# Accumulator copies on VectorE, attention's copies at a higher priority, and two of six weight tiles rounded beside the attention

## The chip, the cores and the metric

The kernel runs on one NeuronCore of a Trainium2 chip: TensorE (PE) multiplies, VectorE (DVE), ScalarE (ACT) and GpSimd (POOL) do the elementwise work, SyncE (SP) issues the DMAs. The metric is the device time of one execution, in microseconds (us); smaller is better.

## The reference, cut to what matters

Windowed attention with a linear position bias on 4 batches of 8 heads, 576 positions, head dimension 64, and then two gated feed-forward layers on the 2304 tokens, all in fp32:

```python
scores = scale * np.matmul(q, k.transpose(0, 1, 3, 2))
scores = np.where(mask, scores + bias[None], -1e9)      # mask: 0 <= q - k < 128
attn = softmax(scores)
x = np.matmul(attn, v)                                  # laid out as [2304, 512]
x = (sigmoid(x @ w_gate) * (x @ w_val)) @ w_out         # 512 -> 1536 -> 512
y = (((x @ w1) * (x @ w2)) @ w3) @ w_out2               # 512 -> 1024 -> 1024 -> 512
```

## The kernel before, in words

**Precision.** A product of two fp32 matrices is made of three matmuls on pairs of a high and a low part (`PASSES`), each part in the type that TensorE takes at full rate. So every operand is split: a copy that rounds makes the high part (`act_copy`, on ACT), a subtraction the low part (`dve_lo` on DVE, `pool_lo` on POOL). The weights come from memory as 64-bit words, 512 KB for a tile of 128x512; `rounded` (L110) turns such a tile into fp32 with one instruction on ACT (L116) and six on DVE (L117 to L122). `convert_next` (L125) takes the next tile of a queue: it rounds it if need be and then either splits it into the weight buffer `wsl` (one ACT copy, one POOL subtraction) or, for an "ahead" tile, writes the fp32 values to a DRAM scratch `early32` (L132), from where a later fetch reads 256 KB of plain fp32. Each call fetches the tile after the next. Buffers of the raw words (`raw`), of the result (`ca`) and of the scale (`cs`) are two each. Conversions run at a priority 300 instructions later than their place in the program (`LATER`).

**Order.** Tokens are in five blocks of 2, 4, 4, 4 and 4 tiles of 128. The attention takes 20 steps (block times pair of heads). Step n issues `stage_p(n-2)` (transposes `pt`, copied to `cp` on ACT at L487, then two selects on POOL), `stage_pv(n-3)` (product `pv`, split into `xt` by ACT and DVE at L514 and L515) and `stage_s(n)` (scores `s`; L450, L453, L459 on DVE, eight exponentials L466 on ACT, L474 on POOL). PE's order in the attention is written out by hand. The other engines' orders come from a planner that takes the ready instruction of the best priority by its own clock; on the chip every engine then works through its queue in that order, so an instruction that waits holds up all behind it. `tc.high_priority(offset=SOONER)` puts an instruction 150 places ahead.

**Fillers.** Between the steps PE gets pieces of the first feed-forward layer for the first group of two hidden tiles: `gv` (the gate and value products, L244; sigmoid on ACT L259, the product of both on DVE L266, its split on ACT and POOL) and `down1` (L283), whose four PSUM tiles `dn` per block go to the accumulator `acc`: the first group copies (L291, on ACT), later groups add on DVE (L293). `FILL` and `READY` say how much and which block at which step. `CONVERT` (L527) says how many tiles `convert_next` takes at a step: twelve in all, six for the first group (hidden tiles 0 and 1) and the six "ahead" tiles of the second group (hidden tiles 2 and 3 of `w_gate`, `w_val`, `w_out`, L192).

**After the attention.** The rest of the fillers runs while the second group's six tiles are fetched and split (L599 to L605); its weight buffers lie where the attention's were. From then on each group is a round of some 74 us over the five blocks, in which DVE, ACT and POOL convert the next group's six tiles and five ahead tiles (`w_out2`, `w3` and others) beside it.

Of the kernel before, what the change touches and what calls it, by code (L numbers as in the profile page):

```python
# [32 lines left out]
SOONER = 150  # L33
# [13 lines left out]
def attn_moe_kernel(  # L47
# [14 lines left out]
    nc = tc.nc  # L62
# [6 lines left out]
    def act_copy(dst, src):  # L69
        nc.scalar.activation(dst, src, AF.Copy)  # L70

    def dve_lo(dst, src, hi):
        nc.vector.tensor_tensor(dst, src, hi.bitcast(F32), ALU.subtract)  # L73
# [13 lines left out]
    def cols(blk):  # L87
        return TILES[blk] * P

    def x_tile(name, blk):  # L90
        return xpool.tile([P, 2, NK, cols(blk)], F32R, name=f"{name}{blk}", tag=f"xb{blk}")

    def acc_tile(blk, shape, name):
        return accpools[blk > 1].tile(shape, F32, tag=f"acc{blk}", name=f"{name}_{blk}")
# [53 lines left out]
    groups = [tuple(range(i, i + GF)) for i in range(0, NF + NM, GF)]  # L148
# [40 lines left out]
    early = [it for it in fold_src if it[0][0] == "o2" or it[0][1] in W3_AHEAD]  # L189
    early += [((i, c), (w1, w2)[c][i - NF]) for c in range(2) for i in groups[NF // GF]]  # L190
    late_n = len(early)
    early += [((i, c), (w_gate, w_val, w_out)[c][i]) for c in range(3) for i in groups[1]]  # L192
    early32 = dpool.tile([P * len(early), DM], F32, name="early32")
    ahead = {key: early32[i * P : (i + 1) * P, :] for i, (key, _) in enumerate(early)}
    ahead_items = [(("ahead", *key), src, None) for key, src in early]
# [33 lines left out]
    def mm_tile(shape, name):  # L229
        mmturn[0] += 1  # L230
        return mmpools[mmturn[0] % len(mmpools)].tile(shape, F32, tag="mm", name=name)
# [40 lines left out]
    def down1(grp, blk, ts):  # L272
        first, last = grp[0] == 0, grp[-1] == NF - 1
        if first:
            acc[blk] = acc_tile(blk, [P, NK, cols(blk)], "acc1")
        if last:
            x2.append(x_tile("x2_", blk))
        for m in range(NK):
            ps = mm_tile([P, TB], f"dn{grp[0]}_{blk}_{m}")[:, 0 : cols(blk)]
            n = 0  # L280
            for i, t in zip(grp, ts):
                for wp, xp in PASSES:
                    nc.tensor.matmul(  # L283
                        ps, wsl[i][:, 2, wp, m * P : (m + 1) * P], t[:, xp],
                        start=n == 0, stop=n == 3 * len(grp) - 1,
                    )
                    n += 1
            a = acc[blk][:, m]
            with tc.high_priority(offset=SOONER):
                if first:  # L290
                    act_copy(a, ps)  # L291
                else:
                    nc.vector.tensor_tensor(a, a, ps, ALU.add)  # L293
            if last:
                act_copy(x2[blk][:, 0, m], a)
                dve_lo(x2[blk][:, 1, m], a, x2[blk][:, 0, m])
            yield 3 * len(grp) * (cols(blk) / 2.4 + 13.3)
# [36 lines left out]
    def attention(actx, conv):  # L334
# [60 lines left out]
        def where(n):  # L395

            blk, pair = divmod(n, NPAIR)
            return pair, blk, TILES[blk], STARTS[blk], min(blk, 1)
# [79 lines left out]
        def stage_p(n):  # L478
            pair, blk, nt, t0, back = where(n)
            s = st[n]  # L480
            for h in range(2):
                ps = gvpool.tile([P, 4, P], F32, tag="mm", name=f"pt{n}_{h}")
                for t in range(nt):
                    nc.tensor.transpose(ps[:, t], s["sm"][:, t // 2 * 2 + h, t % 2], ident)  # L484
                cp = ap2.tile([P, 4, 2, P], F32, tag="cp", name=f"cp{n}_{h}", bufs=4)
                own, prev = cp[:, 0:nt, 1], cp[:, 0:nt, 0]
                act_copy(own, ps[:, 0:nt])  # L487
                nc.gpsimd.affine_select(  # L488
                    out=prev, in_=own, compare_op=ALU.is_gt, fill=0.0, base=0,
                    pattern=[[0, nt], [-1, P]], channel_multiplier=1,  # L490
                )
                nc.gpsimd.affine_select(  # L492
                    out=own, in_=own, compare_op=ALU.is_ge, fill=0.0, base=0,
                    pattern=[[0, nt], [1, P]], channel_multiplier=-1,
                )
                s["cp", h] = cp.rearrange("p t c k -> p (t c k)")

        def stage_pv(n):
            pair, blk, nt, t0, back = where(n)
            s = st[n]  # L500
            ps = gvpool.tile([P, TB], F32, tag="mm", name=f"pv{n}")[:, 0 : nt * P]
            for j in range(-back, nt):
                a, b = max(j, 0) * P, min(j + 2, nt) * P
                m0 = 0 if j < 0 else (2 * j + 1) * P
                for h in range(2):
                    c = slice(h * D, (h + 1) * D)
                    nc.tensor.matmul(  # L507
                        ps[c, a:b], loads[n]["v"][:, j + 1, c], s["cp", h][:, m0 : m0 + b - a],
                        start=j == -back, stop=j == nt - 1, skip_group_check=True,
                    )  # L510
            if pair == 0:
                xt.append(x_tile("xt", blk))
            x = xt[blk]
            act_copy(x[:, 0, pair], ps)  # L514
            dve_lo(x[:, 1, pair], ps, x[:, 0, pair])  # L515

        def fill(budget):

            while fillers and budget > 0:
                cost = next(fillers[0], None)  # L520
                if cost is None:
                    fillers.pop(0)
                else:
                    budget -= cost


        CONVERT = {1: 1, 3: 1, 5: 1, 8: 1, 9: 1, 10: 1, 11: 1, 12: 1, 13: 2, 14: 2}  # L527

        READY = {
            5: (((0,), 0),), 10: (((0,), 1),), 12: (((1,), 0), ((1,), 1)), 14: (((0, 1), 2),), 18: (((0, 1), 3),),  # L530
# [2 lines left out]
            0: ((stage_s, 0),),  # L533
            1: ((stage_s, 1),),
            2: ((stage_s, 2), (stage_p, 0)),
            3: ((stage_s, 3), (stage_pv, 0), (stage_p, 1)),
            4: ((stage_s, 4), (stage_pv, 1), (stage_p, 2)),
            5: ((stage_p, 3), (stage_pv, 2), (stage_s, 5), (stage_pv, 3)),
            6: ((stage_p, 4), (stage_s, 6)),
        }  # L540
# [11 lines left out]
        with tc.manual_schedule(engines={mybir.EngineType.PE}):  # L552
            for n in range(NSTEP + 3):
# [20 lines left out]
                fill(FILL.get(n, FULL))  # L574
                for _ in range(CONVERT.get(n, 0)):
                    with tc.issue_after(st[n]["dve"].ins), tc.issue_after(st[n]["act"].ins):
# [3 lines left out]
    with ExitStack() as conv, ExitStack() as actx:  # L580
        attention(actx, conv)
# [110 lines left out]
```

## Time and profile before

| | us |
|---|---|
| median of three runs | 938.03 (937.9 to 939.07) |
| profiled execution | 936.87 |
| its span, first to last instruction | 935.2 |
| PE busy in the span | 897.4 (96%) |
| DVE, ACT, POOL busy | 565.1, 355.1, 311.6 |

The attention takes the first 197 us of the span. There PE has gaps; behind it PE is busy nearly without one. "Granted clock" is TensorE's clock as a share of 2.4 GHz. Matmuls overlap, so that the start of a row can lie a little before the end of the row above it. A bracket at the end of a timeline row gives the idle time of the engine just before it, and what ended it.

### The profile page before, as it was taken

To read this page: it belongs to the slowest core of one execution; us is meant where nothing else is said; L and a number is where in the kernel's file an instruction comes from. 1 tells how busy PE (TensorE), PEld (TensorE's weight loads), DVE (VectorE), ACT (ScalarE), POOL (GpSimd) and SP (SyncE) were. 2 spreads that over 40 slices of the span, in tenths; PEclk is the share of its full clock that TensorE was granted. 3 is DMA by queue.
4 is the path that set the end of the run, shared out by engine and by line. 5 is a ranking of instruction groups with operands and counts; after the bars stand their busy time and mean duration, and the time that the engine had idled before them with its cause. 6 is when DMAs were issued, how large, how long until landed. Compare 5 with 4: busy or idle time off the path is not lost.

```text
span 935.2 us, 12293 instructions
## 1 busy us (share of the span) xinstructions
PE 897.4 (96%) x4528; PEld 735.1 (79%) x4528; DVE 565.1 (60%) x945; ACT 355.1 (38%) x853; POOL 311.6 (33%) x408
## 2 busy tenths in 40 slices
PE   5889799899999999999999999999999999999998
PEld 2566677678878888888888888888888888888887
DVE  4867787417996996797783468833755524322223
ACT  5778777754322322322331334433322212211110
POOL 4877658452313312412421111104422412411111
PEclk9999899999999999999999999999999999999999
DMA  5544453014351251242130213234300300000113
GB/s 169 170 141 137 145 159 116 26 57 140 109 168 46 91 167 48 68 147 90 55 115 0 68 53 117 91 97 141 111 24 12 101 1 1 23 0 1 46 46 113
DMA packets 32604, 79.71 MB, mean 85 GB/s; under 512 B 3616, under 2 KB 5664, under 8 KB 32544
## 3 DMA queue, kind: packets, MB, share of 16 engines
q1 hardware_dynamic: 32544, 78.92, 26.2%
q8 instruction: 36, 0.59, 0.3%
q14 instruction: 24, 0.20, 0.1%
HBM read 65.27 MB, written 13.63 MB: 84 GB/s over the span
## 4 chain that ended last, share of the span: by engine, by line
PE 72%; DVE 8%; ACT 7%; POOL 6%; DMA 4%; issue 3%; SPq 0%; ACTq 0%; POOLq 0%; DVEq 0%
PE gv L244 43%; PE dn L283 11%; PE o L308 10%; PE w3o L210 4%; ACT sm L466 2%; POOL sm L474 2%; PE s L442 1%; PE pv L507 1%; POOL wsl L76 1%; PE pt L484 1%; POOL cp L488 1%; POOL cp L492 1%; ACT L466 1%; DVE sm L453 1%; DVE s L450 1%
## 5 line engine op out<-in xcount | busy, mean ns | idle before, releaser
L244 PE MATMUL gv<-xt,wsl 128*128 128x512 f32 (+1 forms) x1440 | 308.4, 372 | 7.8 <-ACT acc L70 4.0
L244 PEld LDWEIGHTS gv<-xt,wsl 128*128 128x128 f32 x1440 | 251.9, 190 | 58.2 <-ACT acc L70 4.5
L76 POOL TENSOR_TENSOR gt<-g,gt 128x512 fp32r<-128x512 f32 (+1 forms) x100 | 121.2, 1216 | 427.9 <-ACT gt L70 427.7
L244 PE MATMUL gv<-x,wsl 128*128 128x512 f32 (+1 forms) x960 | 200.2, 368 | 0.0
L244 PEld LDWEIGHTS gv<-x,wsl 128*128 128x128 f32 x960 | 167.6, 189 | 30.2
L266 DVE TENSOR_TENSOR g<-g,gv 128x512 f32<-128x512 f32 (+1 forms) x100 | 62.6, 630 | 168.4 <-PE gv L244 156.3
L283 PE MATMUL dn<-gt,wsl 128*128 128x512 f32 (+1 forms) x720 | 154.9, 369 | 2.4 <-ACT cp L70 1.2
L283 PEld LDWEIGHTS dn<-gt,wsl 128*128 128x128 f32 x720 | 125.7, 188 | 27.2 <-PE dn L283 1.8
L70 ACT ACTIVATE gt<-g 128x512 fp32r<-128x512 f32 (+1 forms) x100 | 58.4, 587 | 145.6 <-DVE g L266 145.6
L259 ACT ACTIVATE g<-gv 128x512 f32<-128x512 f32 (+1 forms) x100 | 54.8, 550 | 150.5 <-PE gv L244 146.4
L308 PE MATMUL o<-wsl,gt 128*128 128x512 f32 x432 | 101.1, 389 | 0.0
L308 PEld LDWEIGHTS o<-wsl,gt 128*128 128x128 f32 x432 | 80.9, 188 | 16.7
L293 DVE TENSOR_TENSOR acc<-acc,dn 128x512 f32<-128x512 f32 (+1 forms) x108 | 66.1, 622 | 20.7 <-PE dn L283 20.5
L474 POOL TENSOR_SCALAR sm<-sm,su 128x128 f32<-128x128 f32 x136 | 53.9, 416 | 21.4 <-DVE su L470 21.2
L466 ACT ACTIVATE sm<-sm,mn 128x128 f32<-128x128 f32 x144 | 56.0, 392 | 7.9 <-DVE mn L459 7.1
L317 DVE TENSOR_TENSOR acc<-acc,o 128x512 f32<-128x512 f32 x54 | 37.1, 688 | 35.2 <-PE o L308 35.2
L442 PE MATMUL s<-ldk,ldq 64*128 64x256 f32 x288 | 41.8, 432 | 7.0 <-DMA ldq<-in_q_dram 4.8
L507 PE MATMUL pv<-cp,ldv 128*64 128x256 f32 (+1 forms) x352 | 40.9, 370 | 4.8 <-POOL cp L492 3.7
L210 PE MATMUL w3o<-wo,w3s 128*128 128x512 f32 x192 | 44.5, 390 | 0.2 <-DVE wo L73 0.2
L210 PEld LDWEIGHTS w3o<-wo,w3s 128*128 128x128 f32 x192 | 36.0, 188 | 8.0 <-DVE wo L73 0.6
L442 PEld LDWEIGHTS s<-ldk,ldq 64*128 64x128 f32 x288 | 29.7, 210 | 14.7 <-issue 10.6
L507 PEld LDWEIGHTS pv<-cp,ldv 128*64 128x64 f32 x352 | 25.7, 149 | 19.7 <-POOL cp L492 6.0
(744 smaller groups left out, 855.3 us busy)
## 6 DMA issues: line engine op xcount, KB each, us to landing
ldk<-in_k_dram SPq DMA_DIRECT2D x16, 320.0 KB, 3.1
ldv<-in_v_dram SPq DMA_DIRECT2D x16, 320.0 KB, 3.1
out_dram<-acc SPq DMA_DIRECT2D x18, 256.0 KB, 2.0
ldq<-in_q_dram SPq DMA_DIRECT2D x16, 256.0 KB, 3.7
w3o<-w3os SPq DMA_DIRECT2D x8, 256.0 KB, 2.8
ldk<-in_k_dram SPq DMA_DIRECT2D x4, 128.0 KB, 2.9
ldq<-in_q_dram SPq DMA_DIRECT2D x4, 128.0 KB, 3.2
raw_(0, 0)_102<-in_w_gate_dram SPq DMA_DIRECT2D x1, 512.0 KB, 5.1
```

The source lines that it names most:

```text
L70: nc.scalar.activation(dst, src, AF.Copy)
L76: nc.gpsimd.tensor_tensor(dst, src, hi.bitcast(F32), ALU.subtract)
L210: nc.tensor.matmul(acc2, w3s[u][:, wp, i * P : (i + 1) * P], wo2[kk][:, xp], start=(kk == 0 and wp == 0 and xp == 0), stop=(kk == NC2 - 1 ...
L244: nc.tensor.matmul(ps, wsl[i][:, s, wp, kk * P : (kk + 1) * P], xs[blk][:, xp, kk], start=(kk == 0 and wp == 0 and xp == 0), stop=(kk == N ...
L266: nc.vector.tensor_tensor(pr, pr, pss[i, 1], ALU.mult)
L283: nc.tensor.matmul(ps, wsl[i][:, 2, wp, m * P : (m + 1) * P], t[:, xp], start=n == 0, stop=n == 3 * len(grp) - 1,)
L293: nc.vector.tensor_tensor(a, a, ps, ALU.add)
L308: nc.tensor.matmul(ps, t[:, xp, tt * P : (tt + 1) * P], wsl[i][:, 2, wp], start=n == 0, stop=n == 3 * len(grp) - 1,)
L442: nc.tensor.matmul(ps[:, h, :, u], ld["q"][r, t * P : (t + 1) * P], ld["k"][r, t * P : (t + 2) * P], start=True, stop=True, skip_group_che ...
L466: s["act"] = nc.scalar.activation(y, y, AF.Exp, bias=mn[:, j : j + 1], scale=1.0 / up, accum_out=su[:, j : j + 1])
L474: nc.gpsimd.tensor_scalar(y, y, su[:, j : j + 1], 1.0, ALU.mult, ALU.mult)
L507: nc.tensor.matmul(ps[c, a:b], loads[n]["v"][:, j + 1, c], s["cp", h][:, m0 : m0 + b - a], start=j == -back, stop=j == nt - 1, skip_group_ ...
```

## The change

The first group's accumulator copies move from ACT to DVE. The attention's copies `cp` and the split of `xt` get the priority of `SOONER`. The ahead tiles of the second group are cut from six to two, (2, 0) and (3, 0): the four others, hidden tiles 2 and 3 of `w_val` and `w_out`, come as raw words behind the attention and are rounded there. The twelve conversions of `CONVERT` become eight: the two ahead tiles stand at steps 12 and 14, the six of the first group stay where they were.

```diff
-    early += [((i, c), (w_gate, w_val, w_out)[c][i]) for c in range(3) for i in groups[1]]
+    early += [((i, c), (w_gate, w_val, w_out)[c][i]) for c in range(1) for i in groups[1]]
...
             with tc.high_priority(offset=SOONER):
                 if first:
-                    act_copy(a, ps)
+                    nc.vector.tensor_copy(a, ps)
...
-                act_copy(own, ps[:, 0:nt])
+                with tc.high_priority(offset=SOONER):
+                    act_copy(own, ps[:, 0:nt])
...
-            act_copy(x[:, 0, pair], ps)
-            dve_lo(x[:, 1, pair], ps, x[:, 0, pair])
+            with tc.high_priority(offset=SOONER):
+                act_copy(x[:, 0, pair], ps)
+                dve_lo(x[:, 1, pair], ps, x[:, 0, pair])
...
-        CONVERT = {1: 1, 3: 1, 5: 1, 8: 1, 9: 1, 10: 1, 11: 1, 12: 1, 13: 2, 14: 2}
+        CONVERT = {1: 1, 3: 1, 5: 1, 8: 1, 9: 1, 10: 1, 12: 1, 14: 1}
```

## Rows read from the trace of the kernel before

**Rows 1.** The page's first part: busy us, share of the span, instructions.
```profile
PE 897.4 (96%) x4528; PEld 735.1 (79%) x4528; DVE 565.1 (60%) x945; ACT 355.1 (38%) x853; POOL 311.6 (33%) x408
```
**Rows 2.** Busy time by stage: length, each engine's busy us, PE clock, DMA share, GB/s.
```profile
75.00:115.00 40.00, 32.94 (x211) 24.61 (x210) 31.17 (x60) 30.97 (x100) 26.80 (x49) 0.88 0.43 141
115.00:200.00 85.00, 78.70 (x505) 58.77 (x504) 50.44 (x96) 60.10 (x182) 48.43 (x94) 0.98 0.30 92
200.00:300.00 100.00, 98.55 (x489) 83.04 (x488) 76.70 (x122) 36.40 (x64) 31.72 (x26) 1.00 0.37 119
```
**Rows 3.** The same view in finer windows.
```profile
110.00:120.00 10.00, 9.16 (x53) 6.96 (x54) 6.54 (x14) 7.94 (x29) 4.79 (x12) 0.71 0.31 98
200.00:220.00 20.00, 20.00 (x111) 17.47 (x110) 6.40 (x13) 10.75 (x19) 9.85 (x8) 1.00 0.39 119
...
290.00:305.00 15.00, 15.00 (x90) 13.38 (x89) 7.33 (x13) 4.90 (x10) 6.58 (x6) 1.00 0.06 25
```
**Rows 4.** Timeline of PE in the attention: start, length, instruction, idle before and releaser.
```profile
86.69 1.37 PE L484 MATMUL pt<-ident,sm 128*128 128x128 f32 x6 [2.01 <-POOL sm L474]
...
105.88 0.93 PE L283 MATMUL dn<-gt,wsl 128*128 128x512 f32 x3 [0.50 <-DVE xt L73]
110.84 2.93 PE L244 MATMUL gv<-xt,wsl 128*128 128x512 f32 x6 [4.04 <-ACT acc L70]
...
130.20 1.20 PE L283 MATMUL dn<-gt,wsl 128*128 128x256 f32 x6 [1.23 <-ACT cp L70]
132.07 0.59 PE L283 MATMUL dn<-gt,wsl 128*128 128x256 f32 x3 [0.68 <-DVE xt L73]
```
**Rows 5.** Timeline of ACT at the longest of these gaps.
```profile
109.63 0.67 ACT L116 ACTIVATE a_('ahead', 3, 0)_1189<-raw_('ahead', 3, 0)_948 128x512 f32<-128x512 f32 x1 [5.05 <-POOL wsl L76]
110.20 1.08 ACT L70 ACTIVATE acc<-dn 128x512 f32<-128x512 f32 x2
```
**Rows 6.** Timeline of PE later in the attention, and behind it.
```profile
164.67 1.66 PE L244 MATMUL gv<-xt,wsl 128*128 128x512 f32 x6 [1.19 <-DVE acc L293]
...
179.93 4.42 PE L244 MATMUL gv<-xt,wsl 128*128 128x512 f32 x18 [1.10 <-ACT g L259]
...
186.60 1.37 PE L484 MATMUL pt<-ident,sm 128*128 128x128 f32 x6 [1.33 <-POOL sm L474]
...
214.62 5.92 PE L244 MATMUL gv<-xt,wsl 128*128 128x256 f32 x48
...
256.05 11.14 PE L244 MATMUL gv<-xt,wsl 128*128 128x512 f32 x48
...
278.71 3.02 PE L244 MATMUL gv<-xt,wsl 128*128 128x512 f32 x12 [0.64 <-DVE g L266]
```
**Rows 7.** Groups by form, 75 to 230 us: name, count, busy us, mean ns, idle before.
```profile
L70 ACT ACTIVATE acc<-dn 128x512 f32<-128x512 f32 x16 | 9.1, 594 | 2.0 <-PE dn L283 2.0
```
**Rows 8.** The line of the second layer's copies: count, ns min/median/max, forms.
```profile
L315 DVE COPY acc<-o x18: 674/691/692, 663.8 to 715.9; 128x512 f32<-128x512 f32 x18
```
**Rows 9.** Timeline of DVE behind the attention.
```profile
224.92 0.41 DVE L266 TENSOR_TENSOR g<-g,gv 128x256 f32<-128x256 f32 x1
...
229.17 1.81 DVE L119 SCALAR_TENSOR_TENSOR a_(5, 0)_2516<-raw_(5, 0)_2500,a_(5, 0)_2516 128x512 uint32<-128x512 uint32 x1
```
**Rows 10.** The same, later.
```profile
269.56 0.42 DVE L117 TENSOR_SCALAR _('ahead', 'o2', 5)_3002<-_('ahead', 'o2', 5)_3002 128x512 f32<-128x512 f32 x1
...
272.39 0.69 DVE L122 TENSOR_TENSOR _('ahead', 'o2', 5)_3002<-_('ahead', 'o2', 5)_3002,_('ahead', 'o2', 5)_3003 128x512 f32<-128x512 f32 x1
...
281.80 0.68 DVE L266 TENSOR_TENSOR g<-g,gv 128x512 f32<-128x512 f32 x1
```
**Rows 11.** Timeline of POOL behind the attention.
```profile
199.69 1.29 POOL L76 TENSOR_TENSOR wsl<-raw_(2, 0)_2158,wsl 128x512 fp32r<-128x512 f32 x1 [4.68 <-ACT wsl L70]
...
229.15 1.29 POOL L76 TENSOR_TENSOR wsl<-a_(4, 0)_2502,wsl 128x512 fp32r<-128x512 f32 x1 [2.54 <-ACT wsl L70]
```
**Rows 12.** DMA issues: KB, median us from issue to landing.
```profile
raw_('ahead', 2, 1)_1056<-in_w_val_dram SPq DMA_DIRECT2D x1, 512.0 KB, 5.5
```

## Prediction

> **What bounds the kernel now.** I read the busy shares first, then the busy time by stage, then PE's timeline where the stages show gaps, then the queues of the engines that end those gaps. PE is busy for 897.4 of 935.2 us [rows 1]; a change that leaves PE's work alone, as this one does, can only move the 38 us in which PE is idle and the time lost to a low clock. The stages say where they are: from 75 to 115 us PE is idle for 40 - 32.94 = 7.1 us at a granted clock of 0.88, from 115 to 200 us for 6.3 us, from 200 to 300 us for 1.45 us [rows 2]. Before 75 us there are hardly any fillers and no accumulator copies; only the priorities touch it.
>
> In PE's timeline most of these gaps have a name [rows 4, 6]. The longest is one event. At 106.8 us PE has made four `dn` tiles and wants a PSUM buffer; it waits 4.04 us, until ACT copies the first of them to `acc`. ACT was not busy: it stood idle for 5.05 us with the rounding of tile (3, 0) at the head of its queue, which needs a `ca` buffer that POOL frees only when it has split tile (1, 2); the copies stood behind it [rows 5]. When PE resumes, six `gv` matmuls take 2.93 us where six of the same form take 1.66 us later [rows 4, 6], and the granted clock of 110 to 120 us is 0.71 [rows 3]: after an idle stretch part of the work ran at the lower level, 1.2 GHz. So this event costs 0.50 + 4.04 + (2.93 - 1.66) = 5.8 us.
>
> **The change part by part.** The sum is made against the profiled execution, 936.87 us (span 935.2 and 1.67 around it); the median of the three runs is 1.16 us more, and what I find is taken off that median.
>
> *The long gap.* The change takes its cause away twice. The copies leave ACT's queue, and tile (3, 0) goes from step 12 to step 14, some 20 us later, when the buffer is long free. On DVE the four copies cost 0.69 us each [rows 8] against 0.59 us on ACT [rows 7], 2.8 us in all, beside four `dn` tiles of three matmuls, for which PE needs 4 x 0.93 = 3.7 us [rows 4]; DVE is busy 31.17 of 40 us there [rows 2], and it loses the rounding of one tile, 3.5 us from the first to the last of its six instructions [rows 10]. What is late next is the softmax chain of the step, whose instructions stand behind the copies on DVE; each is pushed by at most 2.8 us, less than the rounding that goes. I count the whole 5.8 us. Bounds: 4.0 us (only the wait on ACT goes) and 5.8.
>
> *The copies `cp` and `xt`.* Two gaps around 130 us, 1.23 us (`dn` waits for a PSUM buffer until ACT has copied `cp`) and 0.68 us (until DVE has read `pv`) [rows 4], are just such copies standing behind exponentials and roundings. With the priority they come first: 1.9 us. What stands behind a `cp` copy on ACT are the exponentials of the step, delayed by two copies of 0.6 us; they are covered only as long as PE's fillers of the step last. In the steps without fillers, before 75 us, nothing covers them, and the order could cost as much as it gives; I bound that at one gap of the longest kind there, 2.0 us (that ahead of 86.69) [rows 4], either way, and take nothing.
>
> *Roundings that leave the attention.* Four tiles times 3.5 us go from DVE between 100 and 155 us, four instructions of about 0.7 us from ACT, and 4 x (512 + 256) KB of transfers. None of this is PE's work. What it can move are the other gaps: 2.01, 1.19, 1.10 and 1.33 us, 5.6 us together [rows 4, 6]. Each ends with an engine whose queue was full (POOL's normalisation, DVE's adds, ACT's sigmoid), but three of the four lie where no rounding is left now (86 us is ahead of the ahead tiles, 180 and 186 us behind them). Bounds 0 and 5.6; I take a third, 1.9 us, nearer to zero for that reason.
>
> Attention: 5.8 + 1.9 + 1.9 = 9.6 us, between 4.0 and 13.3.
>
> *The four tiles behind the attention.* Here the change pays. First the weights' due times. The raw buffer of (2, 0) comes free when POOL has split it, at 201.0 [rows 11]; the raw words of (2, 1) take up to 5.5 us [rows 12], the rounding 0.7 us on ACT and 3.5 on DVE, the split 0.6 + 1.3 us: ready by 212.6, and (3, 1) one rounding later, by 216.1. PE's `gv` for the second group starts at 214.62 and takes (2, 0) and (3, 0) first, half of its 5.92 us; it asks for (2, 1) at 217.6 and for (3, 1) at 219.1 [rows 6]. So they are hidden, by 3 to 5 us, and the two `w_out` tiles are due only with the `dn` matmuls, behind another `gv` of 11.14 us [rows 6]. DVE has the room up to here: it is busy 6.40 of 20 us from 200 to 220 [rows 3].
>
> Then DVE's queue. From 200 to 300 us DVE is busy 76.70 us [rows 2]. Four tiles add 4 x 3.5 = 14 us at least and the eight copies of the last two blocks 8 x 0.69 = 5.5 us: 96 of 100. And DVE is already late there. The product of hidden tile 3 for the first block ends on PE at 214.62 + 5.92 = 220.5, and DVE takes it (L266) at 224.92, 4.4 us later; for the third block PE ends at 256.05 + 11.14 = 267.2 and DVE takes it at 281.80, 14.6 us later [rows 6, 9, 10]. Between the two DVE rounds twelve tiles, so each lets it fall back by some 10.2 / 12 = 0.85 us. At that lag PE runs out of PSUM buffers: two waits for L266, the first of 0.64 us, which are the 1.45 us of the stage [rows 2, 6]. Four more tiles in the same run make 3.4 us more lag, and all of it is PE's, since PE's waits show that the slack is used up. I take 3.4 us. Bounds: 0, if the planner's order leaves the gaps before 214 us to the four tiles alone, and 9.9 us: 5.5 us of copies, plus four times the 1.1 us by which L119 is longer beside a subtraction on POOL (1.81 against 0.69 us; POOL's begins 0.02 us earlier) [rows 9 to 11].
>
> The Trainium skill, "SBUF — State Buffer", section "Who interferes with whom", says that a DVE instruction with two SBUF inputs and a POOL instruction that reads SBUF exclude each other for the whole length of the one that came first. The pair at 229.15 us agrees [rows 9, 11]. By that rule each of the four moved tiles would meet a subtraction of POOL, 4 x 1.1 = 4.4 us instead of my 3.4, while the moved copies, which read PSUM alone, would never be held.
>
> Sum: -9.6 + 3.4 = -6.2 us. 936.87 - 6.2 = 930.7 for the profiled execution, 931.8 for the median.
>
> **The rivals.**
> *The hole takes the tiles whole.* DVE is idle for 13.6 us between 200 and 220, about what four tiles need; if the lag does not grow and half of the other gaps go, the change gives 5.8 + 1.9 + 2.8 = 10.5 us: 927.5. For it: that idle time [rows 3]. Against: raw words arrive one buffer at a time, and the copies take 5.5 us of the same room. Chance 0.22.
>
> *VectorE becomes the bound behind the attention (the other side).* The price is 9.9 us of waits of `gv` for L266 between 240 and 300 us, against an attention that gives 5.8 + 1.9 = 7.7: 2.2 us slower, 940.2. It decides from the point where the lag of L266 behind PE would pass 14.6 + 7.7 = 22 us. For it: 96 of 100 us busy. Against: from 290 to 305 us DVE is busy only 7.33 of 15 us [rows 3], so the late tiles have somewhere to go. Chance 0.16; with a smaller lag it ends within 0.2% of before.
>
> *Copies placed first wait for PE.* An instruction put early in an in-order queue that arrives before its `pt` or `dn` tile holds up exponentials and softmax. If it takes back 4 us, one gap as long as the one removed, the attention gives 5.6 and the four tiles take 3.4: 2.2 us faster, 935.8. For it: the planner's clock is not the chip's. Against: today's waits of ACT on `pt` are short. Chance 0.14.
>
> **How the numbers follow.** My forecast has the remaining 0.48. A difference under 0.2%, 1.9 us, can't be told from none. Forecast and first rival are faster (0.70, less 0.03 for a forecast that comes out small); the rival of copies placed first is split, 0.07 faster and 0.07 the same; the rival of VectorE is 0.12 slower and 0.04 the same. Faster 0.74, same 0.14, slower 0.12. The range runs from 13.3 us of gain with no loss, 924.7, to 939.5, which leaves out the worse half of the VectorE case.
>
> **What would show it.** Right: no wait of `gv` for `acc` near 106 us and no low clock behind it; `pt` of the last step some 9 us earlier; ACT without a wait for `wsl` of POOL in the attention; behind it PE gaps at L244 released by L266, 4 to 6 us together, within the second group's round, and none on `wsl`. Wrong: the gap comes back at another step, PE waits for the split of (2, 1) or (3, 1), or the waits for L266 pass 9 us.

## The result, and the profile after

The changed kernel takes 945.57 us (median of 10 runs, 941.69 to 948.8) against 938.03 (10 runs, 935.69 to 943.17): a ratio of 1.0083 [1.0066, 1.01], slower by 0.8%. The forecast was 931.8 us, 0.7% faster. The profiled execution took 944.57 us with a span of 942.9, so 7.7 us are to be found between the two traces.

First part of the page, which answers to [rows 1]:

```profile
PE 899.0 (95%) x4528; PEld 735.0 (78%) x4528; DVE 580.9 (62%) x965; ACT 349.0 (37%) x833; POOL 315.7 (33%) x408
```

PE is busy 1.6 us longer than before with the same 4528 matmuls; the rest of the 7.7 us is idle. Busy time by stage, against [rows 2], and in the finer windows of [rows 3]:

```profile
75.00:115.00 40.00, 32.83 (x232) 24.32 (x232) 31.11 (x59) 29.31 (x98) 29.87 (x54) 0.91 0.36 118
115.00:200.00 85.00, 77.28 (x493) 58.63 (x490) 45.17 (x83) 56.85 (x170) 47.68 (x91) 0.98 0.22 69
200.00:300.00 100.00, 94.04 (x453) 78.50 (x452) 89.43 (x142) 32.19 (x54) 29.48 (x21) 0.98 0.37 116
...
110.00:120.00 10.00, 9.79 (x65) 7.65 (x66) 9.83 (x18) 5.25 (x22) 7.04 (x12) 1.00 0.37 110
200.00:220.00 20.00, 20.00 (x111) 17.39 (x110) 17.06 (x28) 8.27 (x14) 6.77 (x5) 1.00 0.32 102
290.00:305.00 15.00, 11.26 (x55) 10.19 (x55) 13.71 (x24) 3.43 (x7) 2.79 (x2) 0.67 0.44 140
```

From 110 to 120 us PE is nearly full at full clock: the long gap is gone. Yet 75 to 115 us holds as much idle time as before (7.2 us), so another gap took its place. And 290 to 305 us, where PE was full and VectorE idle half the time, now has PE idle for 3.7 us at a clock of 0.67, with VectorE nearly full (13.71 of 15 us). PE's timeline in the attention, against [rows 4]:

```profile
80.18 3.01 PE L244 MATMUL gv<-xt,wsl 128*128 128x512 f32 x12
85.70 0.68 PE L484 MATMUL pt<-ident,sm 128*128 128x128 f32 x2 [2.51 <-POOL sm L474]
89.59 0.47 PE L484 MATMUL pt<-ident,sm 128*128 128x128 f32 x1 [3.21 <-POOL sm L474]
90.37 1.60 PE L484 MATMUL pt<-ident,sm 128*128 128x128 f32 x5 [0.30 <-POOL sm L474]
...
110.21 1.66 PE L244 MATMUL gv<-xt,wsl 128*128 128x512 f32 x6 [0.24 <-DVE acc L291]
...
130.66 4.61 PE L244 MATMUL gv<-xt,wsl 128*128 128x512 f32 x12 [2.58 <-DVE acc L293]
```

The six `gv` matmuls at 110.21 take 1.66 us, not 2.93, behind a wait of 0.24 us, not 4.04. But the wait of `pt` for POOL's normalisation, 2.01 us in [rows 4], has become 6.0 us in three pieces. Why, is read from three queues of the changed kernel in that stretch. ACT:

```profile
76.46 0.40 ACT L466 ACTIVATE sm<-sm,mn 128x128 f32<-128x128 f32 x1
...
76.97 1.28 ACT L259 ACT_TABLE_LOAD   x1
...
78.76 1.08 ACT L70 ACTIVATE cp<-pt 128x512 f32<-128x512 f32 x2
79.72 0.61 ACT L70 ACTIVATE xt<-pv 128x512 fp32r<-128x512 f32 x1
...
81.64 0.40 ACT L466 ACTIVATE sm<-sm,mn 128x128 f32<-128x128 f32 x1
...
83.43 0.19 ACT L469 ACTIVATE su<-su 128x4 f32<-128x4 f32 x1
```

DVE:

```profile
81.69 0.68 DVE L73 TENSOR_TENSOR xt<-pv,xt 128x512 fp32r<-128x512 f32 x1
...
84.41 0.68 DVE L450 COPY_PREDICATED s<-mask,s 128x512 f32<-128x512 int32 x1
85.00 0.17 DVE L470 RECIPROCAL su<-su 128x4 f32<-128x4 f32 x1
```

POOL:

```profile
85.27 1.42 POOL L474 TENSOR_SCALAR sm<-sm,su 128x128 f32<-128x128 f32 x4 [0.40 <-DVE su L470]
86.66 2.37 POOL L410 TENSOR_SCALAR tab<-base 128x256 f32<-128x256 f32 x4
89.01 2.43 POOL L474 TENSOR_SCALAR sm<-sm,su 128x128 f32<-128x128 f32 x4
```

On ACT both `cp` copies and the `xt` copy now run ahead of three of the four exponentials of this half step (a step works through its tiles two at a time), so the row sums (L469) come at 83.43; on DVE `xt` and the masks of the next half step run ahead of the reciprocal (85.00); on POOL the position table of the next block (L410) has slipped between the two normalisations. The same points, one row of each engine's timeline, where the early steps have no priority (the run with priorities from step 11, which starts level with the kernel before):

```profile
81.94 0.19 ACT L469 ACTIVATE su<-su 128x4 f32<-128x4 f32 x1
...
82.49 0.17 DVE L470 RECIPROCAL su<-su 128x4 f32<-128x4 f32 x1
...
86.12 1.41 POOL L474 TENSOR_SCALAR sm<-sm,su 128x128 f32<-128x128 f32 x4
...
86.54 1.37 PE L484 MATMUL pt<-ident,sm 128*128 128x128 f32 x6 [2.01 <-POOL sm L474]
...
126.53 3.02 PE L244 MATMUL gv<-xt,wsl 128*128 128x512 f32 x12 [1.90 <-DVE acc L293]
```

ACT is 1.5 us earlier here, DVE 2.5, POOL's second normalisation 2.9, and this takes 1.41 us, not 2.43. The last row answers to the one at 130.66 of the changed kernel, where PE waits 0.7 us longer and the twelve matmuls take 1.6 us more: the granted clock of 130 to 135 us is 0.66 there. PE's filler of that step, 3.0 us from 80.18, was too short by 2.0 us already, so every further delay is PE's.

Behind the attention, PE of the changed kernel:

```profile
212.22 6.17 PE L244 MATMUL gv<-xt,wsl 128*128 128x256 f32 x48
...
277.03 3.02 PE L244 MATMUL gv<-xt,wsl 128*128 128x512 f32 x12 [0.82 <-DVE g L266]
281.29 3.06 PE L244 MATMUL gv<-xt,wsl 128*128 128x512 f32 x12 [1.24 <-DVE g L266]
...
295.83 2.93 PE L244 MATMUL gv<-xt,wsl 128*128 128x256 f32 x12 [2.99 <-DVE g L266]
299.51 2.93 PE L244 MATMUL gv<-xt,wsl 128*128 128x256 f32 x12 [0.75 <-DVE g L266]
302.25 7.16 PE L283 MATMUL dn<-gt,wsl 128*128 128x512 f32 x24
...
320.12 3.04 PE L283 MATMUL dn<-gt,wsl 128*128 128x256 f32 x24
```

And of the kernel before, the rows of the same work from the short block on:

```profile
290.83 5.92 PE L244 MATMUL gv<-xt,wsl 128*128 128x256 f32 x48
296.59 5.63 PE L283 MATMUL dn<-gt,wsl 128*128 128x512 f32 x24
...
312.93 3.04 PE L283 MATMUL dn<-gt,wsl 128*128 128x256 f32 x24
```

The second group begins 2.4 us earlier than in [rows 6] (212.22 against 214.62); the `dn` of the next round's first block comes 7.2 us later (320.12 against 312.93). So 9.6 us are lost between, and hardly anything after. The waits of `gv` for L266 are 5.95 us (with one of 0.15) against 1.45, 4.5 more. After the one of 2.99 us PE runs at the lower clock: twelve matmuls of 128x256 take 2.93 us, where 48 take 5.92 in the kernel before, 1.48 for twelve, and 24 `dn` matmuls 7.16 instead of 5.63. That is 2 x 1.45 + 1.53 = 4.4 us more. DVE says why L266 was late:

```profile
292.55 0.69 DVE L122 TENSOR_TENSOR _('ahead', 'o2', 6)_3098<-_('ahead', 'o2', 6)_3098,_('ahead', 'o2', 6)_3099 128x512 f32<-128x512 f32 x1
294.30 0.43 DVE L117 TENSOR_SCALAR a_(6, 0)_3110<-a_(6, 0)_3110 128x512 f32<-128x512 f32 x1 [1.05 <-ACT a_(6, 0)_3110 L116]
...
295.10 0.68 DVE L266 TENSOR_TENSOR g<-g,gv 128x512 f32<-128x512 f32 x1
```

DVE in the kernel before:

```profile
275.83 0.69 DVE L122 TENSOR_TENSOR _('ahead', 'o2', 6)_3110<-_('ahead', 'o2', 6)_3110,_('ahead', 'o2', 6)_3111 128x512 f32<-128x512 f32 x1
...
289.38 1.27 DVE L266 TENSOR_TENSOR g<-g,gv 128x512 f32<-128x512 f32 x2
```

The round's own five ahead tiles are `o2,0` to `o2,4`; `o2,5`, `o2,6` and (6, 0) are the first of the next round's, which the planner has pulled forward into DVE's queue. In the kernel before `o2,6` was done 16.7 us earlier, and these L266 followed at 289.38. In the changed kernel the roundings ahead of them are still running when PE has reached the short first block of the next round. There it fills a PSUM tile in 1.5 us instead of 3.0.

### The profile page after: what moved, and what is told of

It is laid out like the page before. It is cut to its first block, busy times and chain, and to the rows that moved or that the text cites. A ratio compares the mean times of both kernels' runs of the same rounds, so it can differ in the third digit from the quotient of the medians.

```text
span 942.9 us, 12279 instructions
## 1 busy us (share of the span) xinstructions
PE 899.0 (95%) x4528; PEld 735.0 (78%) x4528; DVE 580.9 (62%) x965; ACT 349.0 (37%) x833; POOL 315.7 (33%) x408
## 4 chain that ended last, share of the span: by engine, by line
PE 70%; DVE 13%; ACT 8%; DMA 4%; issue 3%; POOL 2%; SPq 0%; ACTq 0%; POOLq 0%; DVEq 0%
PE gv L244 42%; PE dn L283 10%; PE o L308 10%; PE w3o L210 4%; ACT sm L466 3%; PE pv L508 2%; POOL sm L474 1%; PE pt L484 1%; ACT cp L70 1%; ACT L466 1%; DVE s L450 1%; DVE sm L453 1%; DVE acc L291 1%; DVE mn L459 1%; ACT xt L70 1%
## 5 line engine op out<-in xcount | busy, mean ns | idle before, releaser
L266 DVE TENSOR_TENSOR g<-g,gv 128x512 f32<-128x512 f32 (+1 forms) x100 | 62.5, 629 | 156.1 <-PE gv L244 140.8
L308 PEld LDWEIGHTS o<-wsl,gt 128*128 128x128 f32 x432 | 80.9, 188 | 16.7
L466 ACT ACTIVATE sm<-sm,mn 128x128 f32<-128x128 f32 x144 | 56.1, 391 | 10.6 <-DVE mn L459 8.5
L484 PE MATMUL pt<-ident,sm 128*128 128x128 f32 x144 | 29.0, 303 | 18.9 <-POOL sm L474 16.6
L484 PEld LDWEIGHTS pt<-ident,sm 128*128 128x128 f32 x144 | 17.9, 144 | 30.8 <-POOL sm L474 26.7
L508 PE MATMUL pv<-cp,ldv 128*64 128x256 f32 (+1 forms) x352 | 38.6, 361 | 3.3 <-ACT g L259 2.4
```

Source lines behind the costliest of these rows:

```text
L266: nc.vector.tensor_tensor(pr, pr, pss[i, 1], ALU.mult)
L308: nc.tensor.matmul(ps, t[:, xp, tt * P : (tt + 1) * P], wsl[i][:, 2, wp], start=n == 0, stop=n == 3 * len(grp) - 1,)
L466: s["act"] = nc.scalar.activation(y, y, AF.Exp, bias=mn[:, j : j + 1], scale=1.0 / up, accum_out=su[:, j : j + 1])
L508: nc.tensor.matmul(ps[c, a:b], loads[n]["v"][:, j + 1, c], s["cp", h][:, m0 : m0 + b - a], start=j == -back, stop=j == nt - 1, skip_group_ ...
```

## The experiments

All were timed in five rounds, each with the kernel before on the same chip (936.65 to 937.65 us). "Second group" is the start of its first `gv` matmuls in the profiled execution, which ends what the attention can give; "waits" are those of `gv` for L266 from 230 to 320 us, "clock" the granted clock from 250 to 310 us.

| run | us | ratio [95%] | second group | waits | clock |
|---|---|---|---|---|---|
| before | 938.03 | 1 | 214.62 | 1.4 | 1.00 |
| changed | 945.57 | 1.0083 [1.0066, 1.01] | 212.22 | 6.0 | 0.91 |
| 1 copies only | 933.23 | 0.9958 [0.9945, 0.9971] | 210.13 | 1.9 | 1.00 |
| 2 priorities only | 936.26 | 0.9985 [0.9975, 0.9995] | 216.11 | 0.5 | 1.00 |
| 3 two tiles only | 940.42 | 1.0033 [1.002, 1.0046] | 208.62 | 7.5 | 0.94 |
| 4 changed, ahead tiles later | 935.02 | 0.9974 [0.9962, 0.9986] | 215.49 | 0 | 1.00 |
| 5 copies and two tiles | 936.7 | 0.9999 [0.9986, 1.0012] | 206.39 | 6.7 | 0.94 |
| 6 the same, ahead tiles later | 928.27 | 0.9913 [0.9899, 0.9927] | 206.35 | 1.5 | 1.00 |
| 7 late copies on ACT | 946.35 | 1.0104 [1.0088, 1.012] | 215.75 | 6.7 | 0.91 |
| 8 before, ahead tiles later | 934.64 | 0.9977 [0.9964, 0.999] | 216.22 | 0 | 1.00 |
| 9 table one step later | 946.16 | 1.0085 [1.0059, 1.011] | 215.21 | 6.2 | 0.91 |
| 10 no priority of `cp` | 943.24 | 1.0062 [1.0038, 1.0086] | 212.77 | 5.5 | 0.91 |
| 11 three ahead tiles | 940.01 | 1.0026 [1.0014, 1.0038] | 213.99 | 3.6 | 1.00 |
| 12 two tiles, ahead tiles later | 931.67 | 0.9934 [0.9916, 0.9953] | 206.67 | 2.2 | 1.00 |
| 13 priorities from step 11 | 937.65 | 1.0008 [0.9997, 1.002] | 206.66 | 6.5 | 0.91 |
| 14 the same, ahead tiles later | 926.93 | 0.9894 [0.9877, 0.9911] | 205.02 | 0 | 1.00 |
| 15 third result buffer | 946.62 | 1.0093 [1.0073, 1.0113] | 216.49 | 5.7 | 0.92 |
| 16 the same as 13, third buffer | 937.6 | 0.9998 [0.9989, 1.0008] | 205.01 | 5.2 | 0.97 |

The changed kernel and runs 4, 7, 9, 11 and 15 have the same attention up to a detail; their second groups start between 212.2 and 216.5 us, 214.9 in the mean (1289.2 / 6). So this column is good to some 2 us, and the trace of the changed kernel is at its early end. The scatter arises ahead of the filler that begins at 80.18 us in the changed kernel: it begins between 80.2 and 84.1 us in these six, and from there to the second group they take 132.0 to 132.5 us. Measured so, runs 13, 14 and 16 take 125.9 us, 5 and 6 take 125.6 and 125.7, the kernel before 133.8 and run 8, with the same attention, 135.4.

Besides that of run 2, the times of runs 5 and 8 came out below what was expected of them, those of 7 and 10 above it.

**1 to 3. Each part alone.** The edit of 1 is the part at L291 of the change's diff, of 2 its two parts with `cp` and `xt`, of 3 those of `early` and `CONVERT`.

> The kernel before with the accumulator copies alone on VectorE; six tiles stay beside the attention, no new priorities. Theory (the loss lies behind the attention, in VectorE's queue, and comes mostly from the four added roundings; the copies add only 5.5 us to that queue): the wait of gv for acc near 106 us shrinks from 4.0 us to under 1, the waits for L266 between 200 and 310 us grow from 1.45 to 2 to 4 us, the time is 932 to 937 us. Rival A (the copies themselves are the load that breaks the queue): waits for L266 of 5 us or more with a low clock behind them, 940 us or more.

> The kernel before with the priorities of cp and xt alone. Theory (the priorities make the new gap of some 6 us ahead of pt at 85 to 91 us, because roundings and splits come to stand ahead of the softmax chain there): that gap appears here too, the long wait for acc near 106 us stays or shifts, nothing changes behind the attention; 939 to 943 us. Rival B (the gap comes from the other two parts): pt waits no longer than the 2.0 us of before at that place, 934 to 938 us.

> The kernel before with two instead of six tiles rounded beside the attention, copies on ScalarE and priorities as before. Theory (the four added roundings overload VectorE's queue in the first round behind the attention): gv waits for L266 between 255 and 310 us for 4 to 7 us, with a low clock behind the last waits; the attention is shorter by 4 to 6 us, since tile (3, 0) no longer blocks ScalarE; 936 to 942 us. Rival A (the copies are the load): waits for L266 of 2 us or less, 931 to 934 us.

The copies alone gain, with no long gap left. The two tiles alone gain 6.0 us at the second group and lose more behind it. Together (run 5) they bring the second group forward by 8.2 us, not by 4.5 + 6.0: in part they cure the same gap. The priorities alone open the gap of `pt` (6.0 us in the same three pieces), as expected, but the time missed: the second group starts 1.5 us later than before, and yet 936.26 us is a little faster. In that trace the long wait for `acc` is gone too, and the waits for L266 are smaller; why the whole gains is not settled. Beside the copies and the tiles the priorities show their price (run 5 against the changed kernel).

**4 to 6. The tiles of the round behind.** The ahead tiles (of `w_out2`, `w3` and others) that the second to fifth rounds take beside their own six are spread otherwise: one instead of five in the first of these rounds.

```diff
-            more = ahead_items[n_ahead * (gi - 1) : n_ahead * gi] if gi < last1 else []
+            cuts = (0, 1, 7, 13, 20)
+            more = ahead_items[cuts[gi - 1] : cuts[gi]] if gi < last1 else []
```

> The changed kernel with four of the five ahead tiles of the first round (w_out2) moved to later rounds: 1, 6, 6, 7 instead of 5, 5, 5, 5. Theory (VectorE's queue in the first round is what costs): the waits for L266 between 255 and 310 us fall under 1 us and the low clock goes with them, 8 to 10 us come back: 935 to 938 us; if the later rounds can't take 12 and 13 tiles, new waits show after 375 us. Rival C (the waits come from where the planner puts L266, not from how much stands in the queue): the waits stay at 4 to 6 us, 942 to 946 us.

> The changed kernel without the priorities of cp and xt: copies on VectorE and two tiles alone. Theory (the priorities make the 6 us gap of pt at 85 to 93 us; the loss behind the attention is of the four added roundings and needs no priorities): pt waits 2.0 us at that place as before, the last 18 gv of the attention start at 175 us or earlier (179.9 before), the waits for L266 between 240 and 310 us stay at 5 to 9 us with a low clock; 938 to 942 us. Rival D (the priorities also set the order behind the attention and so the waits there): waits for L266 under 3 us, 929 to 934 us.

> Copies on VectorE, two tiles, no priorities, and four ahead tiles of the first round moved to later rounds. Theory: the shorter attention of the two parts (5 to 6 us) is kept and no wait for L266 takes it back: 928 to 931.5 us. Rival E (what the attention gains is lost behind it whatever stands in the queue): 935 us or more.

Run 5 leaves the priorities out, run 6 adds the new spread to that. From the changed kernel to 4, 10.6 us go with nothing else changed; from 5 to 6, 8.4. The window of 250 to 310 us of the changed kernel:

```profile
250.00:310.00 60.00, 54.05 (x238) 44.30 (x237) 54.16 (x87) 17.71 (x31) 16.13 (x13) 0.91 0.37 119
```

Of run 4, and then of run 11 (below): PE's idle time, the low clock and VectorE's load go down together.

```profile
250.00:310.00 60.00, 60.00 (x289) 50.62 (x289) 47.40 (x79) 19.59 (x34) 18.48 (x15) 1.00 0.25 80
```

```profile
250.00:310.00 60.00, 56.35 (x267) 46.31 (x266) 51.76 (x83) 18.50 (x32) 18.73 (x15) 1.00 0.29 97
```

**7 and 8. The copies, and the kernel before.** In 7 the copies of the last two blocks go back to ACT; 8 gives the kernel before the new spread.

```diff
-                    nc.vector.tensor_copy(a, ps)
+                    (nc.vector.tensor_copy if blk < 3 else act_copy)(a, ps)
```

> The changed kernel with the copies of the last two blocks back on ScalarE (the first three blocks' stay on VectorE): 5.5 us less in VectorE's queue behind the attention. Theory (the added roundings weigh more than the copies): the waits for L266 fall by 1 to 3 us and stay above 3 us; 940 to 944 us. Rival A (the copies are what breaks the queue): waits under 1.5 us and no low clock, 935 to 938 us.

> The kernel before with four ahead tiles of the first round moved to later rounds. Theory (the queue there is full only with the four added roundings): only the two waits for L266 of 1.45 us go: 935.5 to 937.5 us. Rival F (moving ahead tiles is worth 8 to 10 us by itself, whatever the change did): 931 us or less.

Without the late copies the waits stay (6.7 us; 1 to 3 us less were expected): the tiles make the queue late, not these copies. In the kernel before, the spread is worth 0.2%, against the 1.1% of run 4: the five ahead tiles cost much only together with the four moved ones.

**9 and 10. What opens the gap of `pt`.** 9 was to move POOL's table (`n % NPAIR == NPAIR - 1` instead of `- 2`), 10 takes the priority from `cp` alone.

> The changed kernel with the bias table of the next block made one step later (n % 4 == 3 instead of 2), so that its four POOL instructions of 2.4 us don't stand ahead of the last four normalisations at 86 to 91 us. Theory (with the priorities the queues of POOL and VectorE put other work ahead of the softmax chain, the table being the last of it): the waits of pt at 85 to 93 us fall from 5.7 us to some 3.5; 942 to 944 us. Rival G (POOL's order does not matter there, the chain is late on ScalarE and VectorE already): the waits stay at 5 us or more, 944.5 to 947 us.

> The changed kernel without the priority of the cp copies; the split of xt keeps its own. Theory (two cp copies ahead of the exponentials on ScalarE, and their four selects ahead of the normalisations on POOL, are what delays the softmax chain): the waits of pt at 85 to 93 us fall to 2 to 3 us, the last step's scores start at 161 to 165 us instead of 168 to 171; the waits for L266 behind the attention stay; 936 to 941 us. Rival H (the split of xt does it): waits of 5 us or more stay, 943 to 947 us.

9 is inconclusive: the planner put the table into the same place of POOL's queue, and the gap stayed. How much of it is the table's is open. 10 lies between the two theories: waits of `pt` of 4.2 instead of 6.0 us, so `cp` is a part of the cause, and `xt` another.

**11 and 12. The dose, and two tiles with the spread.** 11 is the changed kernel with `cuts = (0, 3, 9, 14, 20)`; 12 is run 3 with the cuts of run 4.

> The changed kernel with two of the five ahead tiles of the first round moved to later rounds (3, 6, 5, 6). Theory (VectorE's lag grows tile by tile and is paid where the short first block of the next round comes): the waits for L266 between 255 and 310 us fall from 6 to between 1 and 4 us, the low clock partly goes; 937 to 942 us. Rival I (all or nothing): the waits stay at 5.5 us or more, 943 us or more.

> Two tiles beside the attention and four ahead tiles of the first round moved to later rounds; copies on ScalarE, no priorities. Theory (the two-tile part alone shortens the attention by 6 us, and the later ahead tiles take away its price; the copies on VectorE give 2 us more): 929.5 to 932 us. Rival J (the copies on VectorE carry the best version): 934 us or more.

Five, three and one ahead tiles give waits of 6.0, 3.6 and 0 us and 945.57, 940.01 and 935.02 us: some 2.6 us a tile. Run 12 shows that the spread is enough for the two tiles to gain.

**13 and 14. Which steps' priorities.** 13 is the changed kernel with the priority from step 11 on, 14 adds the spread.

```diff
-                with tc.high_priority(offset=SOONER):
+                with tc.high_priority(offset=SOONER if n >= 11 else 0):
                     act_copy(own, ps[:, 0:nt])
...
-            with tc.high_priority(offset=SOONER):
+            with tc.high_priority(offset=SOONER if n >= 11 else 0):
                 act_copy(x[:, 0, pair], ps)
```

> The changed kernel, with the higher priority of cp and xt only for the stages of step 11 and later. Theory (the early steps pay): the gaps of pt at 85 to 93 us fall from 6.0 us to about 2, the scores of the last step start at 161 to 163 us instead of 167.8, L266 is still waited for by 5 to 7 us behind the attention: 935 to 938 us against 945.6 of the changed kernel, level with the kernel before. Rival (the priority costs at any step): the last scores start at 167 us or later and the time is 942 us or more.

> The changed kernel, priority only from step 11 on, and the five ahead tiles of the second group's round moved to the later rounds. Theory: no loss behind the attention and none before 75 us, so 926 to 930 us, level with the run that has no priorities at all (928.3); if the late priorities give the 1.9 us that the prediction counted, 926 to 927. Rival (the priority costs at any step): 931 to 935 us.

Both came as the theory of the early steps had it. The early priorities cost 7.9 us (945.57 to 937.65) and 8.1 us (935.02 to 926.93); the late ones give nothing that can be told (14 against 6, 0.9894 and 0.9913, with intervals that overlap; 13 against 5, 1.0008 and 0.9999).

**15 and 16. A third result buffer.** The trace of the changed kernel shows ACT's L116 waiting for the write of an earlier ahead tile to the scratch, five times for 3.2 to 6.0 us; the L116 that DVE waits for at 294.30 above is one of them. Is it the write or VectorE's work that makes the queue late?

```diff
-        a = spool.tile([P, DM], U32, name=f"a_{key}", tag="ca")
+        a = spool.tile([P, DM], U32, name=f"a_{key}", tag="ca", bufs=3 if len(wpools) > 1 else 2)
```

> The changed kernel with three instead of two result buffers (ca) for the roundings behind the attention; the same tiles at the same places. Theory of the write (the buffer held by the write of an ahead tile makes VectorE's queue late): ScalarE's waits for the write fall under 2 us, the waits of gv for L266 between 250 and 310 us fall from 6.0 to under 3 us with a granted clock of 1.00, and the time to 936 to 940 us. Rival (VectorE's own work, 89 of 100 us busy, makes the queue late): the waits stay at 5 us or more and the time at 943 us or more.

> The same third buffer, with the priority of cp and xt only from step 11 on. Theory of the write: 928 to 933 us against 937.7 of the same kernel with two buffers. Rival (VectorE's own work): 936 us or more.

My theory of the write fell. PE's longest wait in run 15:

```profile
301.03 2.93 PE L244 MATMUL gv<-xt,wsl 128*128 128x256 f32 x12 [3.76 <-DVE g L266]
```

An L116 on ACT ahead of it:

```profile
299.26 0.66 ACT L116 ACTIVATE a_(7, 0)_3124<-raw_(7, 0)_3108 128x512 f32<-128x512 f32 x1 [3.74 <-DMA raw_(7, 0)_3108<-in_w_gate_dram]
```

The window of 250 to 310 us:

```profile
250.00:310.00 60.00, 53.60 (x237) 44.12 (x236) 57.58 (x91) 17.73 (x30) 15.42 (x12) 0.92 0.39 128
```

No L116 there waits for a write any more (they wait for raw words instead), VectorE is busy for 57.58 of 60 us, and the wait for L266 is as long as it was. What is left is VectorE's own work.

## Why the prediction was wrong, step by step

*The long gap: right.* It went as described, with no low clock behind it, and in run 1 without any other part. That the four copies would push the softmax chain by less than the rounding that goes was not measured by itself, but no wait came of it: in runs 5 and 6 the longest wait of PE between 100 and 120 us is 0.56 us.

*The copies `cp` and `xt`: the step that failed.* The prediction counted 1.9 us, said that a step's fillers cover the exponentials which a copy delays, bounded what that costs before 75 us at 2.0 us either way, and took nothing. In the steps up to 10 they do not: the gap of `pt` at 83 to 90 us grew by 4.0 us, and over the whole attention the early priorities cost 8.4 us (the second group at 214.9 in the mean of those six executions against 206.4 and 206.7 in 5 and 13). Counted from the filler at 80 us, from where these executions hardly differ any more, it is 132.2 - 125.9 = 6.3 us: 4.0 in the waits of `pt`, 2.3 at the `gv` of 130.66 (0.7 of wait, 1.6 of clock). The other 2 us lie ahead of it, about what the prediction had bounded there, but it left them out of its lower bound for the attention, 4.0 us. With them, 2.0 us of gain and 9.9 us for the tiles make 945.9 us, and the result lies within; the stated range ended at 939.5.

The late ones gave none of the 1.9 us: from the filler on, run 13 takes 0.3 us more than run 5. The two gaps are gone in run 13, but `gv` now waits 1.90 us for `acc` at 126.53. The prediction's other two terms, 7.7 us together, came out: runs 5 and 6, without the priorities, bring the second group forward by 8.2 us against the trace of before and by 9.8 against run 8. That runs 14 and 16 begin it at 205.0, just the 9.6 us of the sum ahead of before, is luck: run 13, with the same attention, begins it at 206.7, and that difference lies ahead of 80 us.

*The copies wait for PE, the third rival (chance 0.14).* The order of the copies did cost, and twice the 4 us priced. But at the first gap the copies did not wait at all (79.72, behind one another): they ran at once, and what stood behind them was late. Elsewhere ACT's waits for `pt` and `pv` from 75 to 200 us did rise, from 7.6 to 15.3 us; how much of that is cause and how much follows from PE being late, no run told apart.

*Due times: right.* PE of the changed kernel has no wait for a split weight between 200 and 250 us.

*The four tiles: the term that was mis-sized.* 3.4 us were taken, as a lag of 0.85 us per tile; 9.6 us came, 4.5 of waits and 4.4 of low clock, and 0.7 that I did not itemise. The hole of 200 to 220 us did take the work (DVE 17.06 us busy against 6.40 in [rows 3]), but what used to stand there moved back, and with it the whole queue. The row that the prediction used against the second rival, the free DVE of 290 to 305 us, was the place where the late tiles went, and it is no free place: PE then runs the short block, whose PSUM tiles take it 1.5 us each. The lag of L266 could not pass 22 us, the rival's condition: it stayed at 15 (280.56 against 265.3, in the fourth block, which the prediction calls the third), since PE stops when its four buffers are full. A lag that is capped by buffers says nothing of how late a queue is; the waits do.

*VectorE becomes the bound, the second rival (chance 0.16).* This happened. Its price of 9.9 us is met within 0.3 by luck: it was priced as waits, of which 5.95 us came, and the low clock, which it left out, made up most of the rest. The forecast's side of 940.2 was passed because the attention gave 2.4 us, not 7.7.

*The exclusion of DVE and POOL.* A pair like that which the prediction showed at 229 us: L121 at 296.88 us takes 1.65 us in the changed kernel, beside POOL's 1.46 us that began at 296.52. The Trainium skill, "SBUF — State Buffer", section "Who interferes with whom", by which the two exclude each other, agrees with that row. But no run shows these meetings as what makes the queue late, so its 4.4 us stay untested.

*The sum.* -9.6 + 3.4 = -6.2 us was forecast, -2.4 + 9.6 = 7.2 came in the trace. Both failures were in the prediction as prices it named and then took low.

*The signs.* Most of those named for being right came all the same: no wait of `gv` near 106 us, none of ACT for POOL's split, none for a split weight, and 5.95 us of waits for L266 where 4 to 6 were named, though only 2.2 of them at the second group's own matmuls. But `pt` of the last step came 3.6 us earlier (183.05 against 186.60), not 9, and one sign of being wrong came: a gap is back at another step, that of `pt`. The low clock behind the attention is in none of the signs.

## What to carry to other kernels

A priority for one instruction is a delay for all that it passes in an in-order queue: look at each step for the filler that is to cover the delay. Where it was too short the priority cost some 8 us here; where it cost nothing, behind step 11, it gave nothing either. Work moved "into a hole" moves the whole queue behind it; what it costs is read where that queue next meets a short stage, and moving less urgent work out of the same round (here four ahead tiles, 8 to 11 us) can make the move pay. With both mended, run 14 takes 0.9894 [0.9877, 0.9911] of the time before.

## What the runs showed of the hardware that was not expected

Behind one wait of 2.99 us of PE came 4.4 us more of clock: from 300 to 305 us the granted clock of the changed kernel was 0.50, the lower level of 1.2 GHz, with PE at work throughout. In run 11 the longest wait was 1.65 us, and the clock of that stretch 1.00. The length of one wait does not settle it: in run 1 `pv` waited 2.88 us at 142.90, and the clock of 140 to 150 us stayed 1.00. And six executions of one attention, the same up to a detail, ended within 212.2 to 216.5 us; such a scatter is as large as some of the parts that were to be told apart. It arises ahead of 84 us, so that counting from a fixed matmul behind it leaves 0.5 us of it in these six; what makes it was not told apart.
